# A decode layer on one core: TensorE's K stage as a loop of four passes, and the last rows of wq through GpSimd's DMA queue

## The chip, the cores and the metric

The kernel runs on one core of a Trainium2 chip. Time is the device time of one execution in microseconds (us), and the figure quoted for a kernel is the median of its runs. The profile is one execution taken by the hardware profiler. It counts from the first to the last instruction (the span), which is a little less than the execution's device time.

## What is computed

One token for each of four batch entries passes an attention block over a cached window and, beside it, a mixer block; both are added to the input.

```python
xn = layernorm(x)                                   # x: [4, 1, 576]
# attention: 32 query heads, 16 kv heads of 128, the last 2048 of 8192 cached positions
q = xn @ wq                                         # wq: [576, 4096]
p = softmax(q . k_cache[:, :, -2048:] * 128**-0.5)  # per batch entry and head
A = (p @ v_cache[:, :, -2048:]) @ wo                # wo: [4096, 576]
# mixer
h  = gelu(layernorm(xn) @ w1)                       # shifted along the sequence (length 1), then
x1 = xn + shifted(h) @ w2
B  = x1 + gelu(layernorm(x1) @ w3) @ w4             # w3: [576, 4608], w4: [4608, 576]
out = x + A + B
```

All arrays are bf16. The caches' windows are 2 x 33.6 MB and the weights some 21 MB; everything is read once.

## The kernel before, in words

**Order of the work.** There is no planner. Each operation is added to the list of one engine with the events it waits for, an event that it signals and a sort key (`add`, L150; `add_dma`, L154, for transfers). The lists are sorted by key (L533), each engine's signalled operations are numbered, and an event becomes "this engine's semaphore has reached this number" (L535 to L548). A wait for a number that the engine has already waited past is left out (L555). All thresholds are constants, and each engine's program is written out in full: no engine has a loop.

**Transfers.** Nearly all are issued by SyncE, in the order of their keys, from one queue: wq in two loads of 2 MB (rows 0 to 511, L199) and its last 64 rows as 128 half rows of 4 KB (`wqrag`, L203), the K of the 16 kv heads (2 MB each, `issue_k`, L208), V of heads 0 to 3, wo, w1, w2, V of heads 4 to 15 (`issue_v`, L212), w3 in two halves and a rest (L228 to L231), w4 in ten pieces (L238 to L250), the output. ScalarE issues the load of x and half of the output. The K ring (`kring`) and the V ring (`vring`) hold four heads each. K of head g waits for the last transpose of head g - 4, V of head g for the PV product of head g - 4. wq lies in the V ring until q is done, wo, w1 and w2 take the K ring's place after the last transpose, w3 the buffers of the transposed K, w4 the V ring.

**Start.** GpSimd fills the constants (L174 to L193): zeros, identity, permutation, a zeroed `Qpad`. VectorE does the two layernorms (`ln_ops`, L262), and at their end copies the last 64 columns of the normalised x into `ragsrc`, in even places for one half of the columns of wq and in odd ones for the other (L274, L275), to match the half rows of `wqrag`. TensorE transposes x (`pe_xT`), multiplies by wq in five row groups (`pe_q`, L294; the fifth uses `wqrag`), VectorE spreads q into `Qpad` (L310), TensorE transposes the second normalised x (L312) and runs six warm-up products on zeros (`pe_warm`, L315).

**K stage.** 128 groups n of eight transposes (`pe_T`, L324 to L332, 128x128 each, matrix line L330) take K of head n // 8 from the K ring into one of `NTB` = 3 PSUM banks. ScalarE (groups 1, 4 and 7 of each head) or VectorE (the other five) copies a group into one of `NKT` = 12 slots (`evac`, L334 to L337). After two groups of the next head, the scores of a head follow (`pe_SC`, L339, matrix line L346): 16 products of 128x512, each batch entry in its own 32 rows of the output, accumulated over all heads in the four banks `Sps`, since in `Qpad` only the two rows of the current head are not zero. Group n waits for the copy of group n - 3, the scores for all eight copies of their head, a copy for the scores that last used its slot (L351 to L362).

**After it.** Softmax over all heads at once (L365 to L395), PV products head by head (`pe_PV`, L398, matrix line L403), the mixer's small products between them, the products with w3 (`pe_h2`, L487, lines L499, L504 and L508), the second gelu (L514) and the products with w4 (L517, line L424), then the output.

Of the kernel before, what the change touches and what calls it, by code (L numbers as in the profile page):

```python
# [6 lines left out]
BF16 = mybir.dt.bfloat16  # L7
# [5 lines left out]
NKU = 4  # L13
NVU = 4
V_EARLY = 4
NKT = 12
NTB = 3
SC_LAG = 2
ACT_EVAC = (1, 4, 7)
N_WARM = 6  # L20
# [16 lines left out]
def bass_parallel_sum__sliding_block_cached__mixer_s_mlp__decode_kernel(  # L37
    nc, A_x, A_k_cache, A_v_cache, A_wq, A_wo, B_x, B_w1, B_w2, B_w3, B_w4, out
):
    B, Sq, D = A_x.shape  # L40
# [5 lines left out]
    G = Hkv  # L46
    NT = 64
    UE = NT * 128
    NHB = 8 * G
    scale = float(Dh) ** -0.5  # L50
    EPS = 1e-5
    HALF = D // 2
# [5 lines left out]
    with ExitStack() as ctx:  # L58
        def sb(name, shape, dt):
            return ctx.enter_context(nc.sbuf_tensor(name, shape, dt))  # L60
# [7 lines left out]
        regB_t = sb("regB", [128, max(NKT * 1024 + 2 * W, W3E)], BF16)  # L68
        P_sb = regB_t[:, NKT * 1024:NKT * 1024 + W]
        PTc = regB_t[:, NKT * 1024 + W:NKT * 1024 + 2 * W]  # L70
        kring = kring_t[:].rearrange("p (s t d) -> p s t d", s=NKU, t=NT)
# [5 lines left out]
        wqrag = vring_t[:, 4 * Hq * Dh:4 * Hq * Dh + Hq * Dh // 2]  # L77
# [22 lines left out]
        ragsrc = sb("ragsrc", [B, 3, 2, 128], BF16)  # L100
        xnT = sb("xnT", [128, 6, B], BF16)
        xn2T = sb("xn2T", [128, 6, B], BF16)
# [2 lines left out]
        hT_sb = sb("hT_sb", [128, len(HCH), B], BF16)  # L105
        h2T_sb = sb("h2T_sb", [128, 36, B], BF16)
        Qpad_t = sb("Qpad", [128, 130 * G], BF16)
        Qpad = Qpad_t[:, 0:128 * G].rearrange("p (g b c) -> p g b c", g=G, b=B)
        ident_bf = sb("ident_bf", [128, 128], BF16)
        perm_bf = sb("perm_bf", [128, 128], BF16)  # L110
        permT = sb("permT", [128, 128], BF16)
# [3 lines left out]
        zeros_bf = sb("zeros_bf", [128, 512], BF16)  # L115
# [12 lines left out]
        ps = ctx.enter_context(nc.psum_tensor("ps", [128, 8, 512], FP32))[:]  # L128
        Sps = ps[:, 0:4, :]
        tb = [ps[:, 4 + k, :].bitcast(BF16).rearrange("p (t d) -> p t d", t=8) for k in range(NTB)]  # L130
# [10 lines left out]
        H2Tps = ps[:, 7, 0:144].rearrange("p (c b) -> p c b", b=B)  # L141

        S = {}
        for nm in ("pe", "dve", "act", "pool"):
            S[nm] = sem("prog_" + nm)
        prog = {"pe": [], "dve": [], "act": [], "pool": [], "sp": []}
        dma_count = {}
        seqc = [0]

        def add(engine, emit, waits=(), sig=None, key=0.0):  # L150
            seqc[0] += 1
            prog[engine].append(Op(emit, waits, sig, key, seqc[0]))

        def add_dma(pairs, skey, waits=(), key=0.0, engine="sp"):  # L154
            if skey not in S:
                S[skey] = sem("s_" + "_".join(str(k) for k in (skey if isinstance(skey, tuple) else (skey,))))
            dma_count[skey] = dma_count.get(skey, 0) + 16 * len(pairs)

            def emit(e):
                for o_, i_ in pairs:  # L160
                    e.dma_start(o_, i_).then_inc(S[skey], 16)  # L161
            add(engine, emit, waits, None, key)
            return ("dma", skey, dma_count[skey])

        def rag_src(w_ap):
            return w_ap[512:576, :].rearrange("r (h n) -> (r h) n", h=2)
# [15 lines left out]
          waits=["pm1"], sig="perm_bf", key=-96.8)  # L182
        P(lambda e: e.memset(Qpad_t[:], 0.0), sig="qpad_zero", key=-96)
        P(lambda e: e.memset(permT[:], 1.0), sig="pt1", key=-95)
        for b in range(B):
            P(lambda e, b=b: e.affine_select(out=permT[32 * b:32 * b + 32, :], in_=permT[32 * b:32 * b + 32, :], compare_op=ALU.is_equal,
                                             fill=0.0, base=b, pattern=[[-1, 128]], channel_multiplier=4),
              waits=["pt1"] if b == 0 else [f"pt_{b - 1}"], sig="permT" if b == B - 1 else f"pt_{b}", key=-94.9 + 0.01 * b)
# [8 lines left out]
        ev_wq, ev_k, ev_v, ev_w4 = [], [], [], []  # L197
# [2 lines left out]
            ev_wq.append(add_dma([(vring_t[:, 2 * r * Hq * Dh:2 * (r + 1) * Hq * Dh], wq_src[:, 2 * r * Hq * Dh:2 * (r + 1) * Hq * Dh])],  # L200
                                 ("wq", r), (), -20 + r))
        ev_wq = [ev_wq[0], ev_wq[0], ev_wq[1], ev_wq[1]]
        ev_wq.append(add_dma([(wqrag, rag_src(A_wq))], ("wq", 4), (), -15))  # L203

        def kv_src(cache, g):
            return cache[:, g, Sk - W:Sk, :].rearrange("b (i t) d -> i b (t d)", t=NT)
# [31 lines left out]
        for c in range(8):  # L238
            g = G - NVU + c // 3
# [22 lines left out]
        def ln_ops(idx, src, dst, first_waits, tag, k0):  # L262
            add("dve", lambda e: (e.bn_stats(out=stats[:, idx, 0, :], in_=src[:, 0:HALF]),
                                  e.bn_stats(out=stats[:, idx, 1, :], in_=src[:, HALF:D]))[1],
                waits=first_waits, sig=f"{tag}_st", key=k0)
            add("dve", lambda e: e.bn_aggr(out=mv[:, idx, :], in_=stats[:, idx].rearrange("p a s -> p (a s)")),  # L266
                waits=[f"{tag}_st"], sig=f"{tag}_mv", key=k0 + 0.01)
            add("act", lambda e: e.activation(out=sd[:, idx:idx + 1], in_=mv[:, idx, 1:2], func=ACTF.Sqrt, bias=EPS, scale=1.0),  # L268
                waits=[f"{tag}_mv"], sig=f"{tag}_sd", key=k0 + 0.02)
            add("dve", lambda e: e.reciprocal(out=rstd[:, idx:idx + 1], in_=sd[:, idx:idx + 1]),  # L270
                waits=[f"{tag}_sd"], sig=f"{tag}_rstd", key=k0 + 0.03)
            add("dve", lambda e: e.tensor_scalar(out=dst[:], in0=src[:], scalar1=mv[:, idx, 0:1], scalar2=rstd[:, idx:idx + 1],
                                                 op0=ALU.subtract, op1=ALU.mult), waits=[f"{tag}_rstd"], sig=f"{tag}_n", key=k0 + 0.04)
            add("dve", lambda e: (e.tensor_copy(out=ragsrc[:, idx, 0, 0:128:2], in_=dst[:, 512:D]),  # L274
                                  e.tensor_copy(out=ragsrc[:, idx, 1, 1:128:2], in_=dst[:, 512:D]))[1],  # L275
                waits=[f"{tag}_n", "rag_zero"], sig=tag, key=k0 + 0.05)

        def pe_xT(src, idx):
# [28 lines left out]
        for r in range(5):  # L307
# [3 lines left out]
            waits=["q", "qpad_zero"], sig="qT", key=-10)  # L311
# [3 lines left out]
        def pe_warm(e):  # L315
            ins = None
            for w in range(N_WARM):
                ins = e.matmul(ps[:, 4 + (w % NTB), :], lhsT=zeros_bf[:, 0:128], rhs=zeros_bf[:, :], start=True, stop=True)
            return ins
        if N_WARM:  # L320
            add("pe", pe_warm, waits=["zeros_bf"], sig="warm", key=-1)


        def pe_T(n):  # L324
            g, k = n // 8, n % 8

            def f(e):
                ins = None
                for t in range(8):
                    ins = e.transpose(tb[n % NTB][:, t, :], kring[:, g % NKU, 8 * k + t, :], perm_bf[:])  # L330
                return ins
            return f  # L332

        def evac(n):  # L334
            if n % 8 in ACT_EVAC:
                return "act", lambda e: e.activation(out=ktbuf[:, n % NKT], in_=tb[n % NTB], func=ACTF.Copy)  # L336
            return "dve", lambda e: e.tensor_copy(out=ktbuf[:, n % NKT], in_=tb[n % NTB])  # L337

        def pe_SC(g):  # L339
            def f(e):  # L340
                ins = None
                for c4 in range(4):
                    n0 = (8 * g + 2 * c4) % NKT
                    kt = regB_t[:, n0 * 1024:(n0 + 2) * 1024].rearrange("p (t b i) -> p t b i", t=16, b=B)
                    for b in range(B):
                        ins = e.matmul(Sps[32 * b:32 * b + 32, c4, :].rearrange("p (t i) -> p t i", t=16), lhsT=Qpad[:, g, b, :], rhs=kt[:, :, b, :],  # L346
                                       start=(g == 0), stop=(g == G - 1), tile_position=(0, 32 * b))
                return ins
            return f

        for n in range(NHB):  # L351
            w = [ev_k[n // 8]] if n % 8 == 0 else []
            if n == 0:
                w.append("perm_bf")
            if n >= NTB:
                w.append(f"E{n - NTB}")
            add("pe", pe_T(n), waits=w, sig=f"T{n}", key=(n - 0.9) if n % 2 == 1 else n)
            eng, f = evac(n)
            add(eng, f, waits=[f"T{n}"] + ([f"SC{(n - NKT) // 8}"] if n >= NKT else []), sig=f"E{n}", key=n + 0.2)
        for g in range(G):  # L360
            add("pe", pe_SC(g), waits=[f"E{n}" for n in range(8 * g, 8 * g + 8)] + (["qT"] if g == 0 else []), sig=f"SC{g}",
                key=8 * g + 7 + SC_LAG + 0.5)  # L362


        add("dve", lambda e: e.tensor_reduce(out=rmax[:], in_=Sps, axis=AX.XY, op=ALU.max), waits=[f"SC{G - 1}"], sig="rmax", key=KS)  # L365
# [1 line left out]
            waits=["rmax"], sig="negb", key=KS + 0.05)  # L367
        for q in range(4):
# [3 lines left out]
                waits=["negb"], sig=f"exp{q}", key=KS + 0.1 + 0.01 * q)  # L372
            add("dve", lambda e, cs=cs: e.transpose(PTc[:, cs], P_sb[:, cs]), waits=[f"exp{q}"], sig=f"PTc{q}", key=KS + 0.2 + 0.01 * q)  # L373

        for m in range(16):
            q, b = m // 4, m % 4
            w = [f"PTc{q}", "permT"] + ([f"E{NHB - 1 - k}" for k in range(NTB)] + ["xn2T"] if m == 0 else [])
# [154 lines left out]

        for eng in prog:  # L533
            prog[eng].sort(key=lambda op: (op.key, op.seq))
        ev_val = {}  # L535
        for eng in ("pe", "dve", "act", "pool"):
            cnt = 0
            for op in prog[eng]:
                if op.sig is not None:
                    cnt += 1  # L540
                    assert op.sig not in ev_val, op.sig
                    ev_val[op.sig] = (eng, cnt)
# [7 lines left out]
        def emit_program(eng_name, engine):  # L550
            waited = {}
            for op in prog[eng_name]:
                for w in op.waits:
                    s_, v_ = resolve(w)
                    if waited.get(s_.num, 0) >= v_:  # L555
                        continue
                    waited[s_.num] = v_
                    engine.wait_ge(s_, v_)
                ins = op.emit(engine)
                if op.sig is not None:  # L560
                    ins.then_inc(S[eng_name], 1)

        with nc.Block() as block:
            @block.sync
# [46 lines left out]
```

## Time and profile before

| | before |
|---|---|
| median of 9 runs | 220.69 us (220.23 to 221.41) |
| the profiled execution's own time | 221.06 us |
| its span | 219.2 us |
| TensorE: products busy, weight loads busy | 161.3 us, 120.7 us of the span |
| VectorE, ScalarE, GpSimd busy | 74.2, 61.1, 6.0 us |
| bytes moved | 88.90 MB, mean 405 GB/s |
| K stage, first transpose to last scores | 20.5 to 107.7 us |
| PV stage begins | 120.5 us |
| products with w4 | 205.7 to 217.1 us |

Lines name the engine (PE is TensorE, PEld its weight loads, DVE VectorE, ACT ScalarE, POOL GpSimd, SPq SyncE's queue), the operation, `output<-inputs`, and how often it occurs. Brackets show how long the engine had been idle, and what ended that. Products overlap in the array, so busy time of PE isn't PE at its peak. The rows of 40 digits cut the span into equal slices of 5.5 us and give a share in tenths.

### The profile page before, as it was taken

Reading aid. Unit: us, or ns where it says so; the run is one execution under the profiler, and the core shown is the slowest. Engines: PE = TensorE matmul, PEld = TensorE weight load, DVE = VectorE, ACT = ScalarE, POOL = GpSimd, SP = SyncE. Lnnn points to the kernel's source line nnn. Section 1 sums busy time; section 2 is a strip of 40 time slices with the busy share of each in tenths; the row PEclk is TensorE's granted clock in tenths of the full one; section 3 lists DMA queues with packets and bytes.
Section 4 is the critical chain, followed back from the end, with each engine's and each line's share of the span. In section 5 each row is a group of like instructions: output and inputs, shape, how many; then the busy total and the mean of one; then the engine's idle time right before and its main releaser. Section 6 shows DMA issues by size and latency. Waiting matters only on the chain.

```text
span 219.2 us, 6182 instructions
## 1 busy us (share of the span) xinstructions
PE 161.3 (74%) x2918; PEld 120.7 (55%) x2918; DVE 74.2 (34%) x134; ACT 61.1 (28%) x74; POOL 6.0 (3%) x20
## 2 busy tenths in 40 slices
PE   0357899999999999999446853965883345984996
PEld 0353677777777777777201753543563344674663
DVE  5301555556666666666588000330000000000000
ACT  2000655555555555555557100011000000000000
POOL 8200000000000000000000000000000000000000
PEclk9999999999999999999965555555596555695579
DMA  6999999999999999999999999999999999999960
GB/s 240 430 430 427 430 424 427 430 424 420 427 424 421 430 422 427 430 423 427 427 398 414 407 430 424 424 424 430 424 427 427 424 424 435 424 412 407 408 276 27
DMA packets 8577, 88.90 MB, mean 405 GB/s; under 512 B 860, under 2 KB 1256, under 8 KB 3944
## 3 DMA queue, kind: packets, MB, share of 16 engines
q1 hardware_dynamic: 8536, 88.50, 96.1%
q8 instruction: 23, 0.38, 0.7%
q14 instruction: 2, 0.02, 0.0%
q10 hardware_dynamic: 16, 0.01, 0.0%
HBM read 88.49 MB, written 0.00 MB: 404 GB/s over the span
## 4 chain that ended last, share of the span: by engine, by line
PE 44%; DMA 40%; ACT 8%; DVE 4%; issue 2%; SPq 1%
PE ps L330 22%; DMA vring<-in_A_v_cache_dram 18%; DMA regB<-in_B_w_dram 13%; DMA kring<-in_A_k_cache_dram 10%; PE ps L346 8%; ACT regB L336 7%; PE ps L424 5%; PE ps L403 5%; DVE PT L386 2%; PE ps L378 2%; SPq L161 1%; PE ps L499 1%; DVE rmax L365 1%; DVE regB L373 1%; PE ps L508 1%
## 5 line engine op out<-in xcount | busy, mean ns | idle before, releaser
L330 PE MATMUL ps<-perm_bf,kring 128*128 128x128 bf16 x1024 | 66.5, 220 | 2.0 <-DMA kring<-in_A_k_cache_dram 1.6
L330 PEld LDWEIGHTS ps<-perm_bf,kring 128*128 128x128 bf16 x1024 | 57.4, 98 | 15.7 <-issue 6.4
L337 DVE COPY regB<-ps 128x1024 bf16<-128x1024 bf16 x80 | 52.3, 688 | 36.4 <-PE ps L330 34.6
L336 ACT ACTIVATE regB<-ps 128x1024 bf16<-128x1024 bf16 x48 | 47.7, 1022 | 51.5 <-PE ps L330 51.5
L403 PE MATMUL ps<-PT,vring 128*128 128x8 bf16 x1024 | 29.5, 168 | 26.8 <-DMA vring<-in_A_v_cache_dram 24.0
L403 PEld LDWEIGHTS ps<-PT,vring 128*128 128x128 bf16 x1024 | 28.4, 103 | 30.1 <-DMA vring<-in_A_v_cache_dram 25.8
L346 PE MATMUL ps<-regB,Qpad 128*32 128x512 bf16 x256 | 16.7, 382 | 4.2 <-ACT regB L336 4.1
L514 ACT ACTIVATE h2T_sb<-ps 128x144 bf16<-128x144 f32 x1 | 0.3, 291 | 56.6 <-PE ps L508 56.6
L438 DVE TENSOR_TENSOR OTn<-ps,rinvB 128x64 bf16<-128x64 f32 (+2 forms) x3 | 0.6, 203 | 44.6 <-PE ps L403 44.6
L424 PE MATMUL ps<-vring,h2T_sb 128*4 128x288 bf16 x72 | 11.3, 330 | 0.5 <-ACT h2T_sb L514 0.5
L424 PE MATMUL ps<-kring,ORT 128*4 128x288 bf16 x64 | 11.3, 349 | 0.3 <-DVE ORT L442 0.3
L346 PEld LDWEIGHTS ps<-regB,Qpad 128*32 128x32 bf16 x256 | 5.4, 95 | 10.4 <-ACT regB L336 5.4
L378 PE MATMUL ps<-regB,permT 32*128 32x512 bf16 x16 | 5.9, 600 | 5.7 <-DVE regB L373 4.1
L424 PEld LDWEIGHTS ps<-vring,h2T_sb 128*4 128x4 bf16 x72 | 6.9, 97 | 4.7 <-issue 0.5
L424 PEld LDWEIGHTS ps<-kring,ORT 128*4 128x4 bf16 x64 | 6.3, 101 | 4.5 <-DVE ORT L442 0.4
L303 PE MATMUL ps<-xnT,vring 128*128 128x4 bf16 x160 | 4.6, 166 | 5.3 <-DMA vring<-in_A_wq_dram 5.3
L529 DVE CAST out_sb<-ps 4x288 bf16<-4x288 f32 x1 | 0.4, 446 | 22.9 <-PE ps L424 22.9
L268 ACT ACTIVATE sd<-mv 4x1 f32<-4x1 f32 x3 | 0.6, 202 | 25.0 <-DVE mv L266 25.0
L499 PE MATMUL ps<-x1nT,regB 128*128 128x4 bf16 x144 | 5.0, 172 | 3.5 <-DMA regB<-in_B_w_dram 3.5
L303 PEld LDWEIGHTS ps<-xnT,vring 128*128 128x128 bf16 x160 | 4.4, 104 | 5.5 <-DMA vring<-in_A_wq_dram 5.5
L499 PEld LDWEIGHTS ps<-x1nT,regB 128*128 128x128 bf16 x144 | 4.8, 116 | 3.9 <-DMA regB<-in_B_w_dram 3.9
L378 PEld LDWEIGHTS ps<-regB,permT 32*128 32x128 bf16 x16 | 1.1, 99 | 10.5 <-DVE PT L386 5.3
(82 smaller groups left out, 63.8 us busy)
## 6 DMA issues: line engine op xcount, KB each, us to landing
kring<-in_A_k_cache_dram SPq DMA_DIRECT2D x16, 2048.0 KB, 13.5
vring<-in_A_v_cache_dram SPq DMA_DIRECT2D x16, 2048.0 KB, 17.9
kring<-in_A_wo_dram SPq DMA_DIRECT2D x1, 4608.0 KB, 21.1
regB<-in_B_w_dram SPq DMA_DIRECT2D x2, 2304.0 KB, 25.3
vring<-in_B_w_dram SPq DMA_DIRECT2D x8, 576.0 KB, 26.9
vring<-in_A_wq_dram SPq DMA_DIRECT2D x2, 2048.0 KB, 9.6
kring<-in_B_w_dram SPq DMA_DIRECT2D x2, 576.0 KB, 17.2
regB<-in_B_w_dram SPq DMA_DIRECT2D x1, 576.0 KB, 28.8
```

The costliest lines, as they stand in the source:

```text
L161: e.dma_start(o_, i_).then_inc(S[skey], 16)
L303: ins = e.matmul(QTps[:, B * h:B * (h + 1)], lhsT=w, rhs=x_, start=(r == 0 and h == 0), stop=(r == 4), skip_group_check=True)
L330: ins = e.transpose(tb[n % NTB][:, t, :], kring[:, g % NKU, 8 * k + t, :], perm_bf[:])
L336: return "act", lambda e: e.activation(out=ktbuf[:, n % NKT], in_=tb[n % NTB], func=ACTF.Copy)
L337: return "dve", lambda e: e.tensor_copy(out=ktbuf[:, n % NKT], in_=tb[n % NTB])
L346: ins = e.matmul(Sps[32 * b:32 * b + 32, c4, :].rearrange("p (t i) -> p t i", t=16), lhsT=Qpad[:, g, b, :], rhs=kt[:, :, b, :], start=(g = ...
L365: add("dve", lambda e: e.tensor_reduce(out=rmax[:], in_=Sps, axis=AX.XY, op=ALU.max), waits=[f"SC{G - 1}"], sig="rmax", key=KS)
L378: add("pe", lambda e, m=m, q=q, b=b: e.matmul(PTps[m % 4], lhsT=permT[32 * b:32 * b + 32, :], rhs=PTc[32 * b:32 * b + 32, 512 * q:512 * q ...
L386: add("dve", lambda e, o_=o_, i_=i_: e.tensor_copy(out=o_, in_=i_), waits=[f"PTt{m}"], sig=f"PT{m}", key=KS + 0.211 + 0.01 * q + 0.001 * b)
L403: ins = e.matmul(OTps(g)[:, 8 * g:8 * g + 8].rearrange("p (b e) -> p b e", e=2), lhsT=vring[:, g % NVU, t, :], rhs=r_, start=(t == 0), sto ...
L424: return e.matmul(ACC[h], lhsT=lhsT, rhs=rhs, start=start, stop=stop)
L499: ins = e.matmul(H2Tps[:, n, :], lhsT=w3main[:, r, lo:hi:st], rhs=x1nT[:, r, :], start=(r == 0 and n == 0), stop=False, skip_group_check=True)
```

## The change

1. *Loop.* TensorE's K stage becomes `pe_loop`: a body of four heads that runs four times. In it a group waits for a count of semaphores of their own (`ed` for VectorE's copies, `ea` for ScalarE's, `k` for the loads, `qs` for the Q copies) whose threshold is worked out from the pass number in a register. The scores of a pass's last head are run in the next pass behind an `If` (after the loop for the last pass). VectorE and ScalarE first add one pass's worth to `ed` and `ea`, so that the thresholds stay positive. The copies remain written out.
2. *Buffers.* Four PSUM banks and 16 slots instead of three and 12, so that a body of four heads uses the same addresses in each pass.
3. *Q.* The body reads Q from four fixed slots `Qs`. GpSimd copies each head's Q from `Qpad` there, once the scores of the head four before are done. The scores no longer start a new accumulation at head 0; the warm-up products on zeros now write the four score banks and so clear them.
4. *wq.* The load of the last 64 rows moves from SyncE's queue (third there) to GpSimd's, ahead of all GpSimd's other work, with its rows in an order whose slowest dimension is 8. A small load of x into an unused tile `turn` (8 rows of 576 bytes) is issued before it. The copies into `ragsrc` are permuted to match.

```diff
-NKT = 12
-NTB = 3
+NKT = 16
+NTB = 4
+NLU = 4
...
-        ev_wq.append(add_dma([(wqrag, rag_src(A_wq))], ("wq", 4), (), -15))
+        turn = sb("turn", [8, HALF], BF16)
+        add_dma([(turn[:], A_x.rearrange("b s (h d) -> (b s h) d", h=2))], "turn", (), -200, engine="pool")
+        ev_wq.append(add_dma([(wqrag, rag_src(A_wq).rearrange("(i a) n -> a i n", a=8))], ("wq", 4), (), -199, engine="pool"))
...
+            def rag(h):
+                if idx:
+                    return ragsrc[:, idx, h, h:128:2], dst[:, 512:D]
+                return ragsrc[:, 0, h, :].rearrange("b (a j i) -> b j a i", a=4, j=2)[:, h], dst[:, 512:D].rearrange("b (i a) -> b a i", a=4)
...
-                ins = e.matmul(ps[:, 4 + (w % NTB), :], lhsT=zeros_bf[:, 0:128], rhs=zeros_bf[:, :], start=True, stop=True)
+                ins = e.matmul(Sps[:, w % 4, :], lhsT=zeros_bf[:, 0:128], rhs=zeros_bf[:, :], start=True, stop=True)
...
+        LHB = 8 * NLU
+        on_act = [k in ACT_EVAC for k in range(8)]
+        PASS = {"ea": NLU * sum(on_act), "ed": NLU * (8 - sum(on_act))}
+
+        def evac_sem(n):
+            key = "ea" if on_act[n % 8] else "ed"
+            return key, PASS[key] + sum(on_act[k % 8] == on_act[n % 8] for k in range(n + 1))
+
+        def pe_loop(e):
+            with e.Fori(0, G // NLU) as i:
+                def wait_evac(n):
+                    key, val = evac_sem(n % LHB)
+                    e.wait_ge(S[key], i * PASS[key] + (val - (PASS[key] if n < 0 else 0)))
+
+                def scores(u):
+                    e.wait_ge(S["qs"], i * NLU + (u + 1))
+                    for k in range(8):
+                        if k == 7 or not any(on_act[k2] == on_act[k] for k2 in range(k + 1, 8)):
+                            wait_evac(8 * u + k)
+                    pe_SC(e, u % NLU).then_inc(S["sc"], 1)
+
+                for n in range(LHB):
+                    u, k = n // 8, n % 8
+                    if k == 0:
+                        e.wait_ge(S["k", u], i * 16 + 16)
+                    wait_evac(n - NTB)
+                    ins = None
+                    for t in range(8):
+                        ins = e.transpose(tb[n % NTB][:, t, :], kring[:, u, 8 * k + t, :], perm_bf[:])
+                    ins.then_inc(S["tl"], 1)
+                    if k == SC_LAG - 1:
+                        if u == 0:
+                            with e.If(i > 0):
+                                scores(-1)
+                        else:
+                            scores(u - 1)
...
+        def pe_SC(e, u):
...
+                    ins = e.matmul(Sps[32 * b:32 * b + 32, c4, :].rearrange("p (t i) -> p t i", t=16), lhsT=Qs[:, u, b, :], rhs=kt[:, :, b, :],
+                                   start=False, stop=True, tile_position=(0, 32 * b), skip_group_check=True)
...
+        add("act", lambda e: e.sem_inc(S["ea"], PASS["ea"]), key=-1000)
+        add("dve", lambda e: e.sem_inc(S["ed"], PASS["ed"]), key=-1000)
+        add("pe", pe_loop, waits=["perm_bf", "qT", "xn2T"], key=0)
...
+            add(eng, f, waits=[f"T{n}"] + ([f"SC{n // 8 - NKT // 8}"] if n >= NKT else []), sig=f"E{n}", key=n + 0.2, sem_key=evac_sem(n)[0])
...
+            add("pool", lambda e, g=g: e.tensor_copy(out=Qs[:, g % NLU], in_=Qpad_t[:, 128 * g:128 * g + 128].rearrange("p (b c) -> p b c", b=B)),
+                waits=["qT"] + ([f"SC{g - NLU}"] if g >= NLU else []), sig=f"Qs{g}", key=g, sem_key="qs")
...
+        add("pe", lambda e: pe_SC(e, NLU - 1), waits=[f"Qs{G - 1}"] + [f"E{n}" for n in range(NHB - 8, NHB)], sig=f"SC{G - 1}", key=1, sem_key="sc")
```

More of the change, by code (lines that the diff above doesn't have):

```diff
@@ L107, in bass_parallel_sum__sliding_block_cached__mixer_s_mlp__decode_kernel @@
         Qpad_t = sb("Qpad", [128, 130 * G], BF16)
-        Qpad = Qpad_t[:, 0:128 * G].rearrange("p (g b c) -> p g b c", g=G, b=B)
+        Qs = sb("Qs", [128, NLU, B, 32], BF16)
         ident_bf = sb("ident_bf", [128, 128], BF16)
@@ L143, in bass_parallel_sum__sliding_block_cached__mixer_s_mlp__decode_kernel @@
         S = {}
-        for nm in ("pe", "dve", "act", "pool"):
+        for nm in ("pe", "dve", "act", "pool", "tl", "sc", "ed", "ea", "qs"):
             S[nm] = sem("prog_" + nm)
@@ L148, in bass_parallel_sum__sliding_block_cached__mixer_s_mlp__decode_kernel, with add @@
         seqc = [0]
-        def add(engine, emit, waits=(), sig=None, key=0.0):
+        sem_of = {}
+        ev_val = {}
+        def add(engine, emit, waits=(), sig=None, key=0.0, sem_key=None):
             seqc[0] += 1
             prog[engine].append(Op(emit, waits, sig, key, seqc[0]))
+            if sem_key is not None:
+                sem_of[sig] = sem_key
         def add_dma(pairs, skey, waits=(), key=0.0, engine="sp"):
@@ L273, in ln_ops @@
                                                  op0=ALU.subtract, op1=ALU.mult), waits=[f"{tag}_rstd"], sig=f"{tag}_n", key=k0 + 0.04)
-            add("dve", lambda e: (e.tensor_copy(out=ragsrc[:, idx, 0, 0:128:2], in_=dst[:, 512:D]),
-                                  e.tensor_copy(out=ragsrc[:, idx, 1, 1:128:2], in_=dst[:, 512:D]))[1],
+            def rag(h):
+                if idx:
+                    return ragsrc[:, idx, h, h:128:2], dst[:, 512:D]
+                return ragsrc[:, 0, h, :].rearrange("b (a j i) -> b j a i", a=4, j=2)[:, h], dst[:, 512:D].rearrange("b (i a) -> b a i", a=4)
+            add("dve", lambda e: [e.tensor_copy(out=o_, in_=i_) for o_, i_ in (rag(0), rag(1))][1],
                 waits=[f"{tag}_n", "rag_zero"], sig=tag, key=k0 + 0.05)
@@ L317, in pe_warm @@
             for w in range(N_WARM):
-                ins = e.matmul(ps[:, 4 + (w % NTB), :], lhsT=zeros_bf[:, 0:128], rhs=zeros_bf[:, :], start=True, stop=True)
+                ins = e.matmul(Sps[:, w % 4, :], lhsT=zeros_bf[:, 0:128], rhs=zeros_bf[:, :], start=True, stop=True)
             return ins
[L320 to L332, printed above, removed]
+        add("pe", pe_warm, waits=["zeros_bf"], sig="warm", key=-1)
@@ L334, in evac @@
         def evac(n):
-            if n % 8 in ACT_EVAC:
+            if on_act[n % 8]:
                 return "act", lambda e: e.activation(out=ktbuf[:, n % NKT], in_=tb[n % NTB], func=ACTF.Copy)
             return "dve", lambda e: e.tensor_copy(out=ktbuf[:, n % NKT], in_=tb[n % NTB])
[L339 to L349, printed above, removed]
@@ L351, in bass_parallel_sum__sliding_block_cached__mixer_s_mlp__decode_kernel @@
-        for n in range(NHB):
[L352 to L357, printed above, removed]
+        def pe_SC(e, u):
+            ins = None
+            for c4 in range(4):
+                n0 = (8 * u + 2 * c4) % NKT
+                kt = regB_t[:, n0 * 1024:(n0 + 2) * 1024].rearrange("p (t b i) -> p t b i", t=16, b=B)
+                for b in range(B):
+                    ins = e.matmul(Sps[32 * b:32 * b + 32, c4, :].rearrange("p (t i) -> p t i", t=16), lhsT=Qs[:, u, b, :], rhs=kt[:, :, b, :],
+                                   start=False, stop=True, tile_position=(0, 32 * b), skip_group_check=True)
+            return ins
@@ L358, in bass_parallel_sum__sliding_block_cached__mixer_s_mlp__decode_kernel @@
+        add("act", lambda e: e.sem_inc(S["ea"], PASS["ea"]), key=-1000)
+        add("dve", lambda e: e.sem_inc(S["ed"], PASS["ed"]), key=-1000)
+        add("pe", pe_loop, waits=["perm_bf", "qT", "xn2T"], key=0)
+        for n in range(NHB):
             eng, f = evac(n)
-            add(eng, f, waits=[f"T{n}"] + ([f"SC{(n - NKT) // 8}"] if n >= NKT else []), sig=f"E{n}", key=n + 0.2)
+            add(eng, f, waits=[f"T{n}"] + ([f"SC{n // 8 - NKT // 8}"] if n >= NKT else []), sig=f"E{n}", key=n + 0.2, sem_key=evac_sem(n)[0])
+            ev_val[f"T{n}"] = ("tl", n + 1)
+            ev_val[f"E{n}"] = evac_sem(n)
@@ L360, in bass_parallel_sum__sliding_block_cached__mixer_s_mlp__decode_kernel @@
         for g in range(G):
-            add("pe", pe_SC(g), waits=[f"E{n}" for n in range(8 * g, 8 * g + 8)] + (["qT"] if g == 0 else []), sig=f"SC{g}",
-                key=8 * g + 7 + SC_LAG + 0.5)
+            add("pool", lambda e, g=g: e.tensor_copy(out=Qs[:, g % NLU], in_=Qpad_t[:, 128 * g:128 * g + 128].rearrange("p (b c) -> p b c", b=B)),
+                waits=["qT"] + ([f"SC{g - NLU}"] if g >= NLU else []), sig=f"Qs{g}", key=g, sem_key="qs")
+            ev_val[f"SC{g}"] = ("sc", g + 1)
@@ L365, in bass_parallel_sum__sliding_block_cached__mixer_s_mlp__decode_kernel @@
+            ev_val[f"Qs{g}"] = ("qs", g + 1)
+        add("pe", lambda e: pe_SC(e, NLU - 1), waits=[f"Qs{G - 1}"] + [f"E{n}" for n in range(NHB - 8, NHB)], sig=f"SC{G - 1}", key=1, sem_key="sc")
         add("dve", lambda e: e.tensor_reduce(out=rmax[:], in_=Sps, axis=AX.XY, op=ALU.max), waits=[f"SC{G - 1}"], sig="rmax", key=KS)
@@ L534, in bass_parallel_sum__sliding_block_cached__mixer_s_mlp__decode_kernel @@
             prog[eng].sort(key=lambda op: (op.key, op.seq))
-        ev_val = {}
         for eng in ("pe", "dve", "act", "pool"):
@@ L538, in bass_parallel_sum__sliding_block_cached__mixer_s_mlp__decode_kernel @@
             for op in prog[eng]:
-                if op.sig is not None:
+                if op.sig is not None and op.sig not in sem_of:
                     cnt += 1
@@ L560, in emit_program @@
                 if op.sig is not None:
-                    ins.then_inc(S[eng_name], 1)
+                    ins.then_inc(S[sem_of.get(op.sig, eng_name)], 1)
         with nc.Block() as block:
```

## The prediction, made before the changed kernel ran

> **What bounds the kernel now.** I read the DMA rows and queues of the page first.
>
> ```profile
> span 219.2 us, 6182 instructions
> ...
> DMA  6999999999999999999999999999999999999960
> GB/s 240 430 430 427 430 424 427 430 424 420 427 424 421 430 422 427 430 423 427 427 398 414 407 430 424 424 424 430 424 427 427 424 424 435 424 412 407 408 276 27
> ...
> q1 hardware_dynamic: 8536, 88.50, 96.1%
> q8 instruction: 23, 0.38, 0.7%
> ```
>
> From the second slice to the last but two the DMA engines are never idle: the kernel moves bytes at their pace. The second queue is what the change is about: 23 instruction fetches. The trace's packet records (start, duration, size, queue) allow more than the page: on one engine a packet starts a few ns before the end of the one before, so the packets fall into 16 strings, one for each engine. All 16 carry the same data packets (a 16 KB one takes 0.613 us). The 23 fetches, of 16,384 bytes, go round eight strings only: seven get three, one gets two. These seven end at 214.2 to 215.0 us, the eight without at 209.8 to 211.2. A fetch so costs its engine about (214.7 - 210.1) / 3 = 1.53 us, and each transfer, which needs all 16, waits for the fetching eight. (Two 8 KB fetches of another instruction queue lie on two of the other strings, which are the ones that end at 210.7 and 211.2.)
>
> Then the chain of work that ended last, in order of time:
>
> ```profile
> 125.01 1.58 issue
> ...
> 173.40 27.82 DMA regB<-in_B_w_dram
> 201.22 0.05 issue
> 201.27 2.51 PE ps L499 x72
> ...
> 205.72 11.35 PE ps L424 x72
> 217.10 0.40 ACT out_sb L530
> ```
>
> The end is set by the second half of w3 (landed 200.75 by the records), then 18 us of PE work that w4's transfers just keep ahead of (last at 215.0, used at 216.7). So the end moves with w3, and w3 with the slowest string.
>
> Last, the timeline: K stage and SyncE's issues.
>
> ```profile
> 63.77 0.55 PEld L346 LDWEIGHTS ps<-regB,Qpad 128*32 128x32 bf16 x16 [0.39 <-ACT regB L336]
> 63.78 1.05 PE L346 MATMUL ps<-regB,Qpad 128*32 128x512 bf16 x16 [0.22 <-ACT regB L336]
> ...
> 84.07 0.54 SPq L161 DMA_DIRECT2D kring<-in_A_k_cache_dram  x1
> ...
> 122.35 8.01 SPq L161 DMA_DIRECT2D vring<-in_A_v_cache_dram  x4
> ```
>
> A head takes 5.34 us on PE (scores 1.05, 64 transposes 4.3) against 4.9 us of DMA: in this stage PE is the slower, and transfers run on a lead. The last K is issued at 84.07 and reaches the engines about 1.0 us later (first load: issue 0.80, packet 1.83), where the earliest string comes to it at 86.73: slack 1.7 us. V4 is issued at 122.35 after the first PV, and the earliest string comes to it at 125.89: slack 2.5 us. The fetching strings come 1.7 us later to both.
>
> [...]5,870 TensorE records / 256 = 22.9 blocks, 23 fetches. [...]the 1.58 us "issue" above stands at a fetch (record 124.1 to 125.2, PE back at 126.59)[...]. [...] No branch of TensorE is in this trace[...]. [...] No GpSimd DMA is in this trace.
>
> **The change, part by part.**
>
> *Loop.* Before, the K stage has 1,280 matmuls with 1,280 weight loads and some 18 separate waits: 2,578 instructions, 10.1 blocks. The body holds 4 x 64 transposes and 4 x 16 scores with their loads, 640, and 48 waits with one or two register operations each: about 760, 3 blocks; 32 more score instructions come after it. TensorE's program falls from 5,870 to about 4,090, 16.0 blocks, so 15 or 16 fetches, two for each of eight engines, **if** a backward branch finds its block present. Seven of them then carry one fetch less: 1.53 us.
>
> *wq's last rows.* 128 rows of 4 KB: each engine now has 8 packets of 0.159 us = 1.27 us. [...]eight get 1.27 more, eight 1.27 less. [...] Engine numbers aren't in the records: right half -1.27 us for the fetching eight, wrong half +1.27, spread over all 16 zero. I take the right half, since the fetches use exactly eight[...].
>
> *Sum at w3.* Its second half ends at 200.75 on a fetching string with three fetches, 195.6 on a plain one. After: plain 195.6 + 1.27 = 196.9, with the 8 KB fetch 196.9 + 1.27 = 198.2. Fetching: 195.6 - 1.27 + 2 x 1.53 = 197.4, plus idle time if PE issues late. Both kinds meet near 198: that is the next limit.
>
> *PE's lateness.* Start: the eight engines with wq's rows serve them beside the main wq, which lands up to 16 x 0.159 = 2.5 us later. PE's 96 matmuls (13.08, 2.72 us) begin near 15.3, the six warm-up matmuls (2.74 us) end near 21.5, and the first transpose, now at 20.48, follows; the wait for K1 (25.38) takes some back: +0.7 us. Loop: a separate wait is 0.051 us in TensorE's records, so a group of eight transposes (0.53 us on the array) needs one wait, two register operations (taken as the same) and 16 dispatches. PV's 64 pairs in 1.88 us bound a dispatch at 15 ns: 0.15 + 0.24 = 0.39 us, hidden behind 0.53. [...] Behind each register wait stand the next transposes and scores; DVE and ACT wait for those, and SyncE for the last. Sum +1.2 us: below both slacks of before, but strings that are 1.27 ahead and have no fetch yet come to the last K at 85.5, which arrives at 86.3: 0.8 idle. V4 arrives at 124.55, when they get there at 125.4: nothing more. Fetching strings at worst 197.4 + 0.8 = 198.2. So w3 lands at 198.2 to 198.4 for 200.75: **-2.45 us**.
>
> *Together, small or nothing.* Four banks and 16 slots loosen waits of which transposes now show 0.4 us: -0.4 to 0, taken as 0. The 16 Q copies on GpSimd, 0.2 to 0.4 us each (its 128x128 memset takes 0.20), lie in its idle time from 7.2 us on, three heads (16 us) ahead of their scores; uncovered, 0.3 us a head. The two DMAs stand ahead of GpSimd's memsets[...]. The zeroed ragsrc (done 2.50, needed 5.12) and the wait for wq0 (xnT 6.11, used 8.21) hide 4.7 us. The increments on ACT and DVE, 0.05 us, and the permuted ragsrc copies (0.2 us each), +-0.1, lie in the same cover. SyncE loses one issue of 0.41 us, which only lengthens its lead. [...]
>
> Against the profiled execution: 221.06 (span 219.2 and 1.9 around it) - 2.45 = 218.6. The median shown is 0.37 below that execution, so **218.2 us**.
>
> **Rivals.**
>
> 1. *Fetches balanced* (above), 0.62. From 216.8 (12 fetches instead of 16, no lateness) to 219.7 (PE late by 3 us, which eats most of the gain).
>
> 2. *A branch misses* (slower), 0.18: [...]each of the three backward branches waits for a fetch. [...] Price: 2.5 us (record's start to PE's return at 125) to 5.2 us (if the request went out 2.7 us before, as the count of executed instructions at the fetches suggests). Three: 7.5 to 15 us, V4 comes that much later, the slack of 2.5 and about 1.3 from wq's rows go off: 224 to 232, middle 228. For it: the fetch at 124.1 came so late that PE ran dry[...]. [...]
>
> 3. *No saving, no stall, or the wrong half*, 0.13: blocks are fetched again in each pass without stalling PE (three fetches stay, -1.27 us, 219.4), or wq's rows fall on the fetching half (-1.53 + 1.27 = -0.3, 220.4). That is the change not doing what it says.
>
> 4. *The sequencer becomes the bound* (slower), 0.07: register waits at 0.3 us instead of 0.15 make a group 0.54 to 0.65 us, up to 1 us a head, 16 us in all; with 4 us taken as typical, less the slack, 221.5 to 224.
>
> **How the numbers follow.** About 0.2% (0.44 us) is what a measurement of this kernel can tell from no change. Faster: all of 1 and half of 3, 0.68. Same: the other half, 0.07. Slower: 0.25. Likeliest case alone: 216.8 to 219.7. The range runs from 216.8 to 224.0: it holds 1, 3 and 4 and leaves out 2, 0.18.
>
> **What would show it.** Right: 15 to 16 packets on the instruction queue, PE without gaps at heads 4, 8 and 12, w3's wait ending near 198.8 (201.22 now), a GpSimd queue of 0.5 MB, all strings ending within 1.5 us. Wrong: 23 or more fetches; "issue" gaps of microseconds at those heads; a head above 5.5 us; V4's issue later than 125; DMA slices below 400 near 88 and 125 us.

## The result, and the profile after

The changed kernel takes 224.37 us (median of 10 runs, 223.67 to 225.39) against 220.69 us (31 runs of before beside it): ratio 1.0164, 95% interval 1.0146 to 1.0182. It is 1.6% slower where 1.1% faster was forecast, and lies just above the range. The profiled execution took 223.89 us with a span of 222.2.

The DMA rows and queues of the page of after (slices of 5.55 us):

```profile
span 222.2 us, 6383 instructions
...
DMA  6999999999999999999999999999999999999980
GB/s 237 341 328 305 425 428 419 431 428 431 428 432 422 425 425 431 425 431 423 428 421 409 408 429 428 431 422 422 428 425 422 425 428 426 428 421 405 412 335 19
...
q1 hardware_dynamic: 8392, 87.97, 96.0%
q0 software_dynamic: 304, 0.53, 0.7%
q8 instruction: 15, 0.25, 0.5%
```

Two things are to be seen. The instruction queue has 15 packets instead of 23: the loop saves the fetches that were forecast, and passes two to four (47 to 106 us) have one between them, at 69.97 us by the packet records. And slices 2 to 4 show 305 to 341 GB/s where before had 427 to 430, though the DMA row has a 9 there: the engines are busy, but move less. 3 x 430 - (341 + 328 + 305) = 316 GB/s over 5.55 us are 1.75 MB, or 4.1 us at the old rate, lost before 22 us. By the packet records, a 16 KB packet of SyncE's queue, 0.61 us before and afterwards, takes 0.78 to 0.88 us in most of the time in which the last rows of wq are moved (6.9 to 22.1 us), and it does so on all 16 engines: between 9 and 15 us the median of each string of packets lies between 0.80 and 0.88 us.

The timeline of after at the start (start, duration, engine, operation; in brackets what the engine waited for):

```profile
9.32 1.87 PE L314 MATMUL ps<-xnT,vring 128*128 128x4 bf16 x64 [3.96 <-DMA vring<-in_A_wq_dram]
...
17.87 1.87 PE L314 MATMUL ps<-xnT,vring 128*128 128x4 bf16 x64 [6.68 <-DMA vring<-in_A_wq_dram]
...
23.31 1.01 PE L314 MATMUL ps<-xnT,vring 128*128 128x4 bf16 x32 [3.57 <-DMA vring<-in_A_wq_dram]
...
25.05 2.74 PE L329 MATMUL ps<-zeros_bf 128*128 128x512 bf16 x6
...
27.58 4.81 PE L362 MATMUL ps<-perm_bf,kring 128*128 128x128 bf16 x80
```

q is waited for until 23.31; the first transpose runs at 27.58 instead of 20.48. The K stage makes up for nearly all of it, since a head takes 4.94 us (from one score group to the next) instead of 5.34:

```profile
63.45 1.05 PE L382 MATMUL ps<-regB,Qs 128*32 128x512 bf16 x16 [0.22 <-ACT regB L373]
64.43 3.83 PE L362 MATMUL ps<-perm_bf,kring 128*128 128x128 bf16 x64
68.39 1.05 PE L382 MATMUL ps<-regB,Qs 128*32 128x512 bf16 x16
```

The last scores end at 109.1 us instead of 107.7, V4 is issued at 123.80 instead of 122.35, and no engine's string of packets has a gap there. So TensorE's lateness costs nothing; the DMA engines' lost time does. The chain that ended last:

```profile
176.03 28.94 DMA regB<-in_B_w_dram
204.98 0.05 issue
205.02 2.52 PE ps L536 x72
...
209.49 10.51 PE ps L461 x72
220.00 0.02 issue
220.02 0.40 ACT out_sb L567
```

w3 is waited for until 204.98, 3.76 us later than before (201.22); the products with w4 then take 0.84 us less, and 3.0 us remain in the span.

The packets again fall into 16 strings, and show two separate losses. Two strings have neither a fetch nor rows of wq: they end at 213.5 us, and would have ended near 210.1 - 1.25 = 208.8 by the records of before. That is 4.7 us that every engine loses (the slices above show 4.1 of it). The strings with rows of wq alone end at 215.3 to 216.4, those with two fetches alone at 216.1 to 216.6. Two strings have rows of wq and two fetches: 218.6 and 218.7. So the eight engines of wq's rows do overlap the eight fetching ones, in two. These two are last at w3 as well (202.82 and 204.46; the latest fetching string without rows of wq lands at 202.33).

### The profile page after: what moved, and what is told of

It is laid out like the page before. It is cut to its first block, busy times and chain, and to the rows that moved or that the text cites. A ratio compares the mean times of both kernels' runs of the same rounds, so it can differ in the third digit from the quotient of the medians.

```text
span 222.2 us, 6383 instructions
## 1 busy us (share of the span) xinstructions
PE 154.6 (70%) x2918; PEld 120.4 (54%) x2918; DVE 73.4 (33%) x134; ACT 61.1 (28%) x74; POOL 12.2 (6%) x38
## 4 chain that ended last, share of the span: by engine, by line
PE 43%; DMA 41%; ACT 10%; DVE 3%; issue 2%; SPq 1%; POOL 0%; POOLq 0%
PE ps L362 21%; DMA vring<-in_A_v_cache_dram 18%; DMA regB<-in_B_w_dram 13%; DMA vring<-in_A_wq_dram 10%; PE ps L382 8%; ACT regB L373 7%; PE ps L440 5%; PE ps L461 5%; ACT PT L421 2%; DVE PT L423 1%; PE ps L329 1%; PE ps L536 1%; DVE rmax L402 1%; DVE regB L410 1%; PE ps L415 1%
## 5 line engine op out<-in xcount | busy, mean ns | idle before, releaser
L362 PE MATMUL ps<-perm_bf,kring 128*128 128x128 bf16 x1024 | 60.4, 219 | 1.3 <-ACT regB L373 1.3
L382 PE MATMUL ps<-regB,Qs 128*32 128x512 bf16 x256 | 16.8, 382 | 4.2 <-ACT regB L373 4.1
L382 PEld LDWEIGHTS ps<-regB,Qs 128*32 128x32 bf16 x256 | 5.4, 95 | 10.3 <-ACT regB L373 5.4
L461 PE MATMUL ps<-vring,h2T_sb 128*4 128x288 bf16 x72 | 10.5, 311 | 0.5 <-ACT h2T_sb L551 0.5
L461 PEld LDWEIGHTS ps<-vring,h2T_sb 128*4 128x4 bf16 x72 | 6.4, 91 | 4.4 <-issue 0.5
L395 POOL COPY Qs<-Qpad 128x128 bf16<-128x128 bf16 x16 | 4.5, 292 | 75.7 <-PE ps L382 60.4
```

Source lines behind the costliest of these rows:

```text
L362: ins = e.transpose(tb[n % NTB][:, t, :], kring[:, u, 8 * k + t, :], perm_bf[:])
L395: add("pool", lambda e, g=g: e.tensor_copy(out=Qs[:, g % NLU], in_=Qpad_t[:, 128 * g:128 * g + 128].rearrange("p (b c) -> p b c", b=B)), w ...
L461: return e.matmul(ACC[h], lhsT=lhsT, rhs=rhs, start=start, stop=stop)
```

## Experiments

The first theory was that GpSimd's queue slows the engines and that the loop does what was forecast. The rivals: the loop itself costs, or the new row order does it on whichever queue.

**The loop alone.** `loop_only` takes part 4 of the change back:

```diff
-        turn = sb("turn", [8, HALF], BF16)
-        add_dma([(turn[:], A_x.rearrange("b s (h d) -> (b s h) d", h=2))], "turn", (), -200, engine="pool")
-        ev_wq.append(add_dma([(wqrag, rag_src(A_wq).rearrange("(i a) n -> a i n", a=8))], ("wq", 4), (), -199, engine="pool"))
+        ev_wq.append(add_dma([(wqrag, rag_src(A_wq))], ("wq", 4), (), -15))
...
```

The copies into `ragsrc` go back with it.

> The changed kernel with the last rows of wq back on SyncE's queue, third there and in their old row order, and no small load before them: the loop, the buffers and the Q copies alone. Theory 1 (the load through GpSimd slows all 16 DMA engines while it runs; the loop does what was forecast): 15 or 16 instruction fetches, no slice under 400 GB/s before 100 us, second half of w3 landed near 198.7 us, 218.4 to 219.3 us, faster than before by about 1%. Rival (the loop itself costs, through branches, register waits or TensorE's lateness): 222 to 224.5 us, as slow as the changed kernel.

Measured: 219.27 us, ratio 0.9932 (0.9913 to 0.9951). The page of `loop_only`:

```profile
span 217.7 us, 6381 instructions
...
GB/s 242 433 430 427 430 424 424 424 421 430 427 426 430 433 427 424 433 423 421 433 403 413 405 432 430 424 427 424 424 427 424 424 433 429 424 417 402 409 335 29
...
q8 instruction: 15, 0.25, 0.5%
```

No slow slices, 15 fetches. The second half of w3 lands at 199.10, 1.65 us earlier than before, and the time falls by 1.5 us: one fetch of 1.53 us less on the fetching engines. By the packet records the strings without fetches end where they did (209.9 to 211.3 us), and those with two fetches at 213.0 to 213.4, where three fetches gave 214.2 to 215.0. The loop is not the cost; it is a gain.

**The load alone.** `gpsimd_only` is the kernel before with part 4 only.

> The kernel before with only the last rows of wq through GpSimd's queue (with the small load before them, row order and copies as in the changed kernel), no loop. Theory 1: 16 KB packets of SyncE's queue take 0.83 to 0.88 us instead of 0.61 for some 14 us on all engines, the K stage starts some 7 us later, and with three fetches left on the fetching engines the time is 225 to 228 us. Rival (the loop is the cost): 219.5 to 220.5 us.

Measured: 227.0 us, ratio 1.0295 (1.0261 to 1.0330), and slices 2 to 4 at 367, 315 and 333 GB/s:

```profile
GB/s 234 367 315 333 443 428 419 419 425 434 406 411 416 405 405 364 384 390 421 434 425 406 410 416 431 428 428 425 419 428 428 425 428 420 442 419 395 412 329 34
```

This is more than the changed kernel's loss. A head takes its old 5.3 us there, the late start isn't made up for, V4 is issued at 128.93, and the row has slices of 364 to 405 GB/s between 73 and 101 us, where K is issued too late. The loss itself is in part 4; this run doesn't yet say in what of it.

**GpSimd's queue with the old row order.** `pool_natural` is the changed kernel without the small load and with the old order of the rows (and of the copies into `ragsrc`):

```diff
-        ev_wq.append(add_dma([(wqrag, rag_src(A_wq).rearrange("(i a) n -> a i n", a=8))], ("wq", 4), (), -199, engine="pool"))
+        ev_wq.append(add_dma([(wqrag, rag_src(A_wq))], ("wq", 4), (), -199, engine="pool"))
```

> The changed kernel with the last rows of wq still through GpSimd's queue, but in their old row order (slowest dimension 128, so on 16 engines) and without the small load. Theory 1 (GpSimd's queue slows the engines whatever the row order): slices of 300 to 350 GB/s stay for as long as the load runs; with 8 rows an engine instead of 16 about half as long, so 2 to 2.5 us lost, 220.5 to 222.5 us. Theory 2 (the row order does it[...]): no slow slices, 218.3 to 219.3 us.

Measured: 219.69 us, ratio 0.9954 (0.9935 to 0.9974), 0.4 us above what theory 2 gave. Packets stay at 0.61 us while the load runs (5.6 to 10.8 us), and no slice is slow:

```profile
GB/s 242 434 431 425 422 422 431 422 434 422 432 431 431 422 428 431 428 417 425 434 409 414 407 436 434 416 416 425 428 431 428 425 431 429 430 421 393 410 340 39
```

The first theory falls: with the old row order GpSimd's queue slows nobody.

**The new row order on other queues.** `act_k8` issues the load of the change from ScalarE, `sp_k8` from SyncE in its old third place, both without the small load:

```diff
-        ev_wq.append(add_dma([(wqrag, rag_src(A_wq).rearrange("(i a) n -> a i n", a=8))], ("wq", 4), (), -199, engine="pool"))
+        ev_wq.append(add_dma([(wqrag, rag_src(A_wq).rearrange("(i a) n -> a i n", a=8))], ("wq", 4), (), -99, engine="act"))
```

> The changed kernel with the last rows of wq in the row order of the change (slowest dimension 8) but issued from ScalarE's queue, and without the small load. Theory 1: no slow slices beyond the bytes moved (16 KB packets of SyncE's queue stay near 0.61 to 0.65 us), 217.5 to 220 us, by whether its eight engines are the fetching ones. Theory 2 (row order): packets of 0.8 us and more on all engines while it runs, 222 to 225 us.

> The changed kernel with the last rows of wq in the change's row order but issued from SyncE in its old third place, no small load: no second queue to alternate with. If the slowing needs the alternation of two queues on the same engines over 14 us, it shrinks to the time of the load itself, 1.3 us more on eight engines and little on the others: 219.3 to 221.2 us, the upper end if these engines are also fetching ones. If the row order slows all engines by the same sum of time wherever it stands: 222.5 to 225 us.

Measured: `act_k8` 223.76 us (ratio 1.0151, 1.0125 to 1.0177), `sp_k8` 224.23 us (1.0155, 1.0127 to 1.0183). In `act_k8` packets take 0.78 to 0.82 us for most of 14 us; in `sp_k8` 1.42 to 1.48 us, from 13 to 18 us. The row of `sp_k8` (the second) shows a shorter and deeper dip:

```profile
GB/s 238 342 322 357 429 426 426 420 429 426 426 422 426 432 432 438 426 425 426 429 408 410 410 426 429 426 423 423 426 426 423 429 423 424 435 421 401 411 340 18
```

```profile
GB/s 239 435 252 310 430 430 430 427 424 430 427 425 424 427 421 415 424 430 428 430 410 410 409 428 421 435 430 421 418 427 424 433 433 422 422 424 403 408 298 14
```

2 x 430 - (252 + 310) = 298 GB/s over 5.57 us: 1.66 MB, nearly the 1.75 of after; `act_k8` loses 1.49 MB by the same sum. So the row order costs much the same (3.5 to 4.1 us at 430 GB/s) whichever queue it is on and however long it is spread.

**What in the row order.** Three readings were left: the writing (neighbouring partitions to one index of the slowest dimension), the concentration on eight engines (eight strings carry the rows in the changed kernel), the strided reading. `pool_a16` and `pool_a32` keep GpSimd's queue and the striding, with 16 and 32 as the slowest dimension (the copies of x permuted to match), without the small load; `pool_blk8` keeps 8 as the slowest dimension and reads 64 KB in one piece for each index (from other rows of wq, so it does not compute this part of q):

```diff
-rag_src(A_wq).rearrange("(i a) n -> a i n", a=8)
+rag_src(A_wq).rearrange("(i a) n -> a i n", a=16)    # pool_a16; a=32 in pool_a32
...
+A_wq[0:512, :].rearrange("r (h n) -> (r h) n", h=2).rearrange("(a s) n -> a s n", a=8)[:, 0:16, :]    # pool_blk8
```

> The changed kernel with the last rows of wq through GpSimd's queue, rows strided as in the change but with 16 as the slowest dimension instead of 8 (16 engines[...]), no small load, copies of x permuted to match. Theory 2a (any row order that gives an engine neighbouring partitions slows the others): 16 KB packets of 0.75 us and more on all engines while it runs, 220.5 to 222.5 us. Theory 2b (the concentration on eight engines does it): packets stay at 0.61 us, 218.8 to 220.2 us as with the old row order.

> The changed kernel, eight engines as in the change, but the load reads eight blocks of 16 successive half rows each, 64 KB an engine, instead of strided half rows. It reads other rows of wq, so the last rows' part of the product is wrong; bytes, queue and destination are those of the change. Theory 2c (the strided reading in HBM does it): packets stay at 0.61 to 0.65 us, 217.5 to 220 us. Theories 2a and 2b (destination or concentration): 0.80 to 0.88 us for some 14 us, 223.5 to 225.5 us as the changed kernel.

> The changed kernel with the last rows of wq through GpSimd's queue, strided as in the change but with 32 as the slowest dimension: 16 engines, groups of 4 neighbouring partitions[...]. [...]16 KB packets at 0.61 us, second half of w3 landed near 199.2 us, 219.2 to 220.1 us. Rival (any strided order slows the engines, in proportion to what one engine carries): packets of 0.75 us and more between 5.5 and 12 us, 220.4 to 221.5 us.

| run | slowest dimension | neighbouring partitions in a group | 16 KB packet while the load runs | w3's second half landed | ratio (95%) |
|---|---|---|---|---|---|
| changed kernel | 8, strided | 16 | 0.78 to 0.88 us, some 14 us | 204.46 us | 1.0164 (1.0146 to 1.0182) |
| pool_blk8 | 8, in blocks | 16 | 0.72 to 0.86 us, some 14 us | 203.72 us | 1.0159 (1.0127 to 1.0191) |
| pool_a16 | 16, strided | 8 | 0.81 to 0.85 us, 7 us | 200.91 us | 1.0006 (0.9991 to 1.0022) |
| pool_a32 | 32, strided | 4 | 0.61 us | 199.16 us | 0.9937 (0.9921 to 0.9954) |
| pool_natural | 128 | - | 0.61 us | 199.22 us | 0.9954 (0.9935 to 0.9974) |

The rows of `pool_a16`, then of `pool_a32`:

```profile
GB/s 240 340 381 428 431 428 431 428 425 431 428 423 428 425 431 422 431 429 428 428 411 410 410 424 431 422 428 431 422 425 428 428 425 428 427 427 397 409 350 42
```

```profile
GB/s 242 430 435 428 425 428 425 425 422 431 428 429 431 425 431 422 431 423 431 431 402 414 407 435 431 413 425 428 428 428 428 425 428 432 420 424 399 408 343 37
```

`pool_blk8` takes the striding away and stays slow (0.72 to 0.86 us). `pool_a16` takes the concentration away: by its packet records all sixteen strings carry wq's rows, eight each, and they are slowed in the same way (0.81 to 0.85 us), half as long (7 us for 14). Neither is needed for the loss. `pool_a32` reads in strides on sixteen engines, again eight rows each, and slows nobody (0.61 us). What is left is the writing: one index of the slowest dimension holds 16, 8 or 4 neighbouring partitions, and the loss is there with 16 and 8 and not with 4. That is read from the access patterns; the packet records name neither engines nor partitions.

**The small load.** `no_turn` is the changed kernel without it.

> The changed kernel without the small load of x ahead of wq's last rows. The slowing of all engines stays (0.80 to 0.88 us for some 14 us), since the row order is the same: 222 to 225 us. What it adds is where the eight engines lie: [...]the strings that carry wq's rows overlap the fetching ones in two or in six engines, and the last transfers end near 216.4 or 218.6 us by that; if no engine overlaps, the time is at the lower end.

Measured: 223.84 us (two runs, 223.31 and 224.37), ratio 1.0142 (1.0084 to 1.0200). The slowing stays. The difference from the changed kernel is inside what two runs can tell. In its profile two strings end apart from the rest here too, at 218.0 and 218.1 us, as two do in the changed kernel (and in `act_k8`, at 217.8 and 218.0), so this one execution shows no effect of the small load on where the eight engines lie. Whether it has one in others isn't settled.

**The buffers alone.** `banks_only` is the kernel before with `NKT = 16` and `NTB = 4`, written out (its first transpose also waits for q and the second transposed x).

> The kernel before with only the four PSUM banks and 16 slots, all written out: 23 fetches, wq as before. The end is set by the DMA engines and not by TensorE: a head takes 4.95 us instead of 5.34, V4 is issued some 5 us earlier, and the time stays within 0.3% of before (220.2 to 221.2 us). Rival (part of the loop's 1.5 us came from the banks): 219.2 to 220.0 us.

Measured: 220.60 us, ratio 0.9990 (0.9976 to 1.0004): no difference. The timeline of `banks_only` shows a head in 5.04 us, with 23 fetches:

```profile
61.62 1.05 PE L346 MATMUL ps<-regB,Qpad 128*32 128x512 bf16 x16 [0.29 <-DVE regB L337]
62.59 3.77 PE L330 MATMUL ps<-perm_bf,kring 128*128 128x128 bf16 x64
66.66 1.05 PE L346 MATMUL ps<-regB,Qpad 128*32 128x512 bf16 x16 [0.29 <-DVE regB L337]
```

So most of the faster K stage (0.30 of 0.40 us a head) comes from the buffers. It is worth nothing by itself, since the DMA engines set the end: V4 is issued at 117.67, 4.7 us earlier than before, and the second half of w3 still lands at 200.69 (200.75 before). The 1.5 us of `loop_only` come from the fetches. In the changed kernel the faster K stage hides TensorE's late start, as the comparison with `gpsimd_only` suggests; no run has the new row order with the buffers alone.

## Why the prediction was wrong, point by point

- **What bounds the kernel** was right: the DMA engines, and of them the eight that fetch instructions. Each part's effect is seen at w3's landing, and `banks_only`, which speeds TensorE alone, changes nothing.
- **Loop: right.** 15 fetches (15 or 16 forecast). `loop_only` lands w3 at 199.10; the loop's term alone gives 195.6 + 2 x 1.53 = 198.7. Rival 2 (a branch misses) didn't come: no gap of over 0.6 us between weight loads from the second pass to the end of the loop, and one fetch in passes two to four. The 23 fetches of before came to one for 255 TensorE records (5,870 / 23); a pass has some 681, 2.7 times that. So no later pass fetched its whole body again; how much TensorE keeps was not shown.
- **The term that failed** is *wq's last rows*: "eight get 1.27 more, eight 1.27 less". It counted the bytes of each engine and took the other engines' packets to keep their 0.613 us. They did not: in the new row order every engine's packets take 0.17 to 0.27 us longer for some 14 us. Instead of -1.27 us the fetching engines got +3.1 (they end near 216.3, in `loop_only` at 213.0 to 213.4), and the two that carry wq's rows as well +5.4 (218.6). w3's landing shows the latter: 204.46 - 199.10 = +5.4 us. Without the overlap in these two it would have landed at 202.33, so 2.1 of the 5.4 us are the overlap and 3.2 the slowing, net of the 1.27 us of rows that these engines no longer carry. Neither the range's bounds for this term (-1.27 to +1.27) nor a rival contained that; 224.37 us lies among the times given to rival 2, for another reason.
- **Right half or wrong half:** neither. Six of wq's eight engines are plain ones and two fetch. The argument from "exactly eight" was too weak, and nothing shows that the small load moves wq's rows to other engines (`no_turn`). The strings, forecast to end within 1.5 us of each other, end between 213.5 and 218.7.
- **PE's lateness** was put at +0.7 us at the start; the other 0.5 of the sum of 1.2 us was for the loop's branches, which no trace of before showed. q's wait was priced from bytes too: TensorE's last 96 products were put near 15.3 and ran at 17.87 and 23.31, so the first transpose came 7.1 us late. The larger buffers, taken at 0, and the loop gave back 0.4 us a head. Both were wrong in size and by luck nearly cancelled: V4 was issued 0.25 us after the forecast time (123.80 for 123.55).
- **Rival 4** didn't come: a register operation takes 0.032 or 0.037 us in the records (medians of its two kinds), a branch 0.145 us (median of eight), and a head in the loop takes 4.94 us, less than the 5.04 of the same banks written out.

**The cause, and what stays open.** The row order is shown as the cause, on three queues: with 16 neighbouring partitions to one index of the slowest dimension SyncE's 16 KB packets took 0.72 to 0.88 us beside the load on GpSimd's or ScalarE's queue and 1.42 to 1.48 with the load on SyncE's own, with 8 they took 0.81 to 0.85, with 4 they kept their 0.61. By what mechanism was not shown: the packet records don't say which engine writes which partitions. Nor does a run here tell why all 16 engines slow down by about the same amount (medians of 0.80 to 0.88 us a string between 9 and 15 us).

**A version that beats both.** `loop_only` at 219.27 us (ratio 0.9932) and `pool_a32` at 219.22 us (0.9937) are the fastest; their intervals overlap, so wq's place in the queues makes no difference that these runs can tell. Part 4 is best left out.

## What to carry to other kernels

Where the DMA engines set the end, look for what single engines carry beside the data: each fetch of TensorE's instructions cost its engine an estimated 1.53 us here (from the ends of the strings of before), and a loop that saved eight of 23 was worth 0.7%. Before reordering a load to move bytes between engines, ask how many neighbouring partitions one index of its slowest dimension covers: with four the 16 KB packets beside the load kept their 0.61 us here, with eight or sixteen they took 0.72 to 0.88 us on GpSimd's queue for most of the time that it ran. And price a transfer beside others by a measured pair of the same shape, not by its bytes.

## What of the hardware was not expected

- A load of 512 KB (0.6% of the bytes) took 3.5 to 4.1 us of all engines' time, with 16 neighbouring partitions to one index of its slowest dimension, from three different queues.
- Passes two to four of the loop had one fetch, though a pass is 640 matmuls and weight loads and about 41 register operations and branches (165 over four passes), 2.7 times the 255 records to a fetch of before. TensorE's records hold 20 separate semaphore waits in the whole program, against 32 before: most of the 48 waits on register thresholds in a pass have no record of their own.
- The first pass does stall once: 1.54 us pass from one weight load to the next at 36.2 us in the changed kernel, at a fetch that runs from 35.1 to 36.2 us. `loop_only` has the same pause at 31.0 us (1.6 us).
